# Four loads and transposes put elsewhere in a written order: attention with a relative bias, then a snake MLP

## The chip, the cores and the metric

The kernel runs on 1 core of one Trainium2 chip. The metric is the device time of one execution in microseconds (us); lower is better. Several executions are timed, and one more is run under the hardware profiler: its time, its span and its trace belong together.

## The reference

Attention over 8 batch elements, 8 heads, 576 positions and 64 channels a head, with a bias that depends on the distance of two positions alone; then, on the 8 x 576 = 4608 tokens of 512 channels that come out, a two-layer MLP of width 2048 with the activation h + sin(alpha h)^2 / alpha.

```python
scores = q @ k.transpose(0, 1, 3, 2) / np.sqrt(64) + bias      # bias[h, |i - j|], 32 buckets
attn = np.exp(scores - scores.max(-1, keepdims=True))
attn = attn / attn.sum(-1, keepdims=True)
x = (attn @ v).transpose(0, 2, 1, 3).reshape(4608, 512)
h = x @ w_in                                                   # 512 -> 2048
g = h + np.sin(alpha * h) ** 2 / alpha
out = g @ w_out                                                # 2048 -> 512
```

## The kernel before, in words

**Work and names.** The kernel records tasks, and a table called `ORDER` (a string, from line 343 on) lists them by short names, one after the other. Each task goes to one engine, and an engine runs its tasks in just that order, so each engine's queue is the table with the other engines' names left out. A number behind a slash is the PSUM bank (of eight), and a letter there another engine than the usual one. The names, with t the batch element (0 to 7), p the pair of heads (0 to 3), and b a block of 512 tokens (0 to 8):

- `n` t p kind: GpSimd loads the natural rows of k (kind 0) or q (kind 1) of one pair into a part of `xT` that is not used yet (L581, 144 KB). For t up to 2, TensorE turns them (`t` t p kind, L703) and a copy (`c`, L651 or L653) brings them to `kT` and `qT`. From t = 3 on, `g` stages a whole element in HBM (L608) and `k` turns it by a DMA of SyncE (L614).
- `v` t c and `y` t a: GpSimd loads the values. A `v` is 128 of the first 512 positions (L587, 128 KB), a `y` the last 64 positions for one head of each pair (L593, 32 KB). There are two sets of value tiles, so those of element t wait for the last product of element t - 2 that reads the set.
- `T`, `X`, `S`: scores on TensorE (L766, L720, L749, L725); `E` their exponential on ScalarE (L774), `B` the bias as a product on VectorE (L797 and neighbours).
- `A` t p w: probabilities times values for half the rows of a pair (L805 with `y`, then L810 with the four `v`); `L` t: the same for the last 64 rows of all pairs (L821). `N` and `NL` divide by the sum on VectorE (L842, L843), into tiles `xp` and `xl`.
- `Y` t p: SyncE turns an `xp` tile into `xT` by a DMA (L850), the columns of the first 512 positions of element t; `YL` t: two such DMAs (L861) bring its last 64 positions. For t = 0, TensorE and a copy do this.
- `I` b.f: 4 matmuls of the first layer (L887) that read 512 tokens of `xT`; `Z` the sine on ScalarE (L893), `Q` the square (L898 on ScalarE, L900 on VectorE), `G` the sum (L905). `O`: the second layer (L915), `W` its eviction (L651 or L653), `D` its store (L928). `wi` and `wo` load the weights (L598, L603).

**Order around the change.** TensorE does scores, products and both layers mixed, in one stream. Block 2 of the MLP, tokens 1024 to 1535, needs the last 128 tokens of element 1 and the first 384 of element 2: so `Y20` to `Y23` and `YL1`, but not `YL2`, whose tokens 1664 to 1727 belong to block 3.

**Queues.** GpSimd issues its loads one after the other, and so does SyncE its transposes and stores. Each of GpSimd's DMAs has one of eight semaphores in turn, and its issue waits until the DMA eight places before it has landed. A task that waits holds up all that stands behind it on its engine.

```python
    def turn_x(self, xcell, t, p):
        n0 = S * t
        self.nc.sync.dma_start_transpose(
            out=self.xT[:, p, n0:n0 + 512].rearrange("d (c s) -> d c s", c=4),
            in_=xcell["x"][:, :, :].rearrange("s c d -> s (c d)"))
```

Of the kernel before, what the change touches and what calls it, by code (L numbers as in the profile page):

```python
# [348 lines left out]
X00r/6 ET0300 n101 BT0210 BT0200 T0110/2 t111/5 n231 BT0000 ET0110 T0011/0 n130 t121/4 BT0001 c111
ET0011 n200 X01r/2 BT0010 c121 m0 EX00r X00q/0 BT0201 BT0110 m1 BT0101 EX01r BT0100 X01q/4 wi1  # L350
T0311/6 BX00r EX01q BT0011 A000/3 n210 BT0300 A010/2 EX00q n220 N000 A001/5 m3 BT0211 ET0311
t110/4 N010 m2 t101/3 T0111/0 c110/A N001 T0301/6 n120 ET0111 BX01r T0310/4 c101 n230 A020/2
ET0301 BT0111 wi2 A021/3 N020 T1000/0 ET0310 wi0 S0/7 N021 t130/6 y11 t231/2 ET1000 BT0301 T1001/4
BX00q A011/3 BT0311 wi3 ES0 c231 c130/A X10r/0 y10 ET1001 A030/7 BT0310 N011 v12 P00/6 BS0 EX10r
P02/2 A031/3 N030 v11 BX01q T1011/4 Y02/A N031 t220/7 ET1011 n221 T1100/0 Y00 T1300/2 c220 P01/6
ET1100 P03/5 Y01 t120/4 BT1011 t210/7 ET1300 T1010/0 c120 L0/6 ET1010 Y03 wo0 t230/4 NL0 t200/5
T1311/2 c200 T1301/0 I0.8/6 ET1311 c230 ET1301 S1/5 c210 X11r/2 v10 I0.0/4 BT1000 EX11r BT1100 v13
I0.3/7 ES1 Z0.0 BS1 BT1010 I0.9/5 BT1300 PL0/3 I0.7/2 YL0 n211 Z0.9 Q0.0 I0.1/3 wo1 Z0.3 Q0.9 G0.0
Z0.7 I0.12/1 v21 Q0.3/A G0.9 I0.2/4 wo2 Z0.8 G0.3 Q0.7/A I0.5/5 n201 Q0.8 Z0.2 G0.7 I0.14/7 Z0.1
Q0.2 Q0.1/A G0.8 I0.10/2 Z0.12 wo3 G0.2 I0.13/6 Q0.12/A BX10r g31 G0.1 Z0.10 I0.4/4 BT1001 Z0.14  # L360
# [24 lines left out]
BT3111 I2.0/3 BT3201 v43 ET3010 A300/1 I2.14/0 ET3200 BT3010 BT3301 N300 I2.5/7 Z2.0 D6 BT3101
BT3200 I2.13/6 BT3211 o4 I2.2/1 Z2.14 A310/5 Q2.14 Z2.2 D4 Q2.0 O7.12 Q2.2/A N310 I2.3/4 Z2.5 G2.0
I2.1/5 Q2.5/A G2.2 Z2.13 G2.14 A311/3 O7.14 G2.5 Z2.1 I2.6/1 Q2.13 Q2.1/A G2.13 Z2.3 I2.7/7 BS3
G2.1 I2.11/6 Z2.7 Q2.3 Z2.6 N311 I2.4/5 G2.3 Q2.7/A A301/3 Q2.6/A W7 I2.15/4 Z2.11 G2.6 D7 Q2.11/A
I2.12/2 G2.7 Z2.15 BX31r I2.9/1 Z2.4 G2.11 Q2.15/A BX30q I2.8/7 N301 Z2.9 Q2.4 Y30 I2.10/6 Q2.9/A
G2.15 Z2.8 G2.4 O8.0/3 Z2.12 D5 O8.2 G2.9 A330/0 Q2.8/A Z2.10 X40r/4 Y31 G2.8 A320/1 EX40r N330  # L390
O8.4 Q2.10 O8.6 N320 O9.0/7 G2.10 O9.2 T3310/0 Q2.12 T3210/4 O9.4 ET3310 G2.12 O10.0/6 ET3210
O10.2 O8.8 T3311/0 BT3210 T4200/4 O8.10 ET3311 A321/2 ET4200 BT3311 O8.12 O10.4 N321 T4300/0
BT3310 T4201/4 Y32 O8.14 ET4300 A331/2 W8 ET4201 L3/1 N331 T4011/4 Y33 NL3 v51 T4010/2 O9.6 ET4011
BX40r O9.8 y50 D8 ET4010 X41r/0 v50 O9.10 T4001/4 EX41r y51 T4211/2 O10.6 YL3 ET4001 v40 O10.8
O10.10 y40 ET4211 T4100/0 T4101/4 O9.12 v53 ET4100 O9.14 k50 v52 O10.12 W9 ET4101 O10.14 BT4200
T4000/0 T4110/2 T4301/4 ET4000 I3.3/7 ET4110 BT4000 S4/1 I3.15/0 BT4001 k51 ES4 W10 ET4301 A400/3
# [584 lines left out]
```

## Time and profile before

| what | value |
|---|---|
| timed runs, median of 3 | 380.35 us (380.34 to 381.17) |
| profiled execution, its own time | 381.76 us |
| its span | 379.9 us |
| TensorE (PE) busy | 365.4 us, 96% |
| ScalarE (ACT) busy | 310.5 us, 82% |
| VectorE (DVE) busy | 265.3 us, 70% |
| GpSimd (POOL) busy | 86.0 us, 23% |
| mean granted TensorE clock | 0.991 |

All times in the profile are counted from the start of the span. "Idle before" names the event that ended an engine's wait. A matmul's end is modelled, so rows of TensorE overlap a little. POOL's rows of L581, L587 and L593 are the issues of its loads; SPq rows are the issues of SyncE. The landing of a DMA is a number of its own, counted from the start of its issue. The granted clock is the share of full speed that TensorE had.

### The profile page before, as it was taken

To read this page: it belongs to the slowest core of one execution; us is meant where nothing else is said; L and a number is where in the kernel's file an instruction comes from. 1 tells how busy PE (TensorE), PEld (TensorE's weight loads), DVE (VectorE), ACT (ScalarE), POOL (GpSimd) and SP (SyncE) were. 2 spreads that over 40 slices of the span, in tenths; PEclk is the share of its full clock that TensorE was granted. 3 is DMA by queue.
4 is the path that set the end of the run, shared out by engine and by line. 5 is a ranking of instruction groups with operands and counts; after the bars stand their busy time and mean duration, and the time that the engine had idled before them with its cause. 6 is when DMAs were issued, how large, how long until landed. Compare 5 with 4: busy or idle time off the path is not lost.

```text
span 379.9 us, 9143 instructions
## 1 busy us (share of the span) xinstructions
PE 365.4 (96%) x3769; PEld 195.6 (51%) x3769; DVE 265.3 (70%) x613; ACT 310.5 (82%) x417; POOL 86.0 (23%) x104
## 2 busy tenths in 40 slices
PE   4879999999998899999999999999999999999996
PEld 3567445654464455544554555445654564444453
DVE  4789899639975496389754985596729866769412
ACT  5979998999899599899988989999899855686301
POOL 8894682048208000600000050500000000000000
PEclk9989999999999899999999999999999999999999
DMA  9999999999999992890254078980130032020005
GB/s 174 217 170 184 186 193 158 126 201 145 157 131 142 172 100 57 93 155 21 98 129 97 0 83 135 141 69 28 40 89 3 2 83 92 2 83 0 2 29 193
DMA packets 140889, 39.68 MB, mean 104 GB/s; under 512 B 126208, under 2 KB 136304, under 8 KB 140848
## 3 DMA queue, kind: packets, MB, share of 16 engines
q0 software_dynamic: 92864, 18.45, 60.0%
q1 hardware_dynamic: 46272, 18.61, 23.5%
q10 hardware_dynamic: 1712, 2.04, 1.6%
q8 instruction: 29, 0.48, 0.5%
q14 instruction: 12, 0.10, 0.1%
HBM read 36.89 MB, written 15.34 MB: 137 GB/s over the span
## 4 chain that ended last, share of the span: by engine, by line
PE 88%; DMA 6%; ACT 2%; POOL 1%; issue 1%; SPq 1%; DVE 1%; POOLq 0%
PE acc L915 33%; PE acc L887 31%; PE acc L810 8%; PE acc L766 8%; PE acc L805 2%; DMA xT<-xp 2%; DMA v<-in_v_dram 2%; PE acc L821 2%; DMA xT<-in_k_dram 2%; DMA toep<-e_sb 1%; ACT s L893 1%; PE acc L720 1%; PE acc L703 1%; POOL xT L581 1%; PE acc L749 1%
## 5 line engine op out<-in xcount | busy, mean ns | idle before, releaser
L915 PE MATMUL acc<-w_out,g 128*128 128x512 f16 (+1 forms) x592 | 144.3, 374 | 0.0
L887 PE MATMUL acc<-xT,w_in 128*128 128x512 f16 x576 | 135.8, 381 | 2.8 <-DMA xT<-xp 2.2
L774 ACT ACTIVATE u<-acc 128x1024 f16<-128x1024 f32 x128 | 123.7, 1034 | 12.2 <-PE acc L766 11.3
L893 ACT ACTIVATE s<-acc,alphaT 128x512 f16<-128x512 f32 x144 | 91.9, 682 | 23.6 <-PE acc L887 23.0
L905 DVE SCALAR_TENSOR_TENSOR g<-s,inv_a,acc 128x512 f16<-128x512 f16 x144 | 103.2, 742 | 7.3 <-ACT s L898 5.7
L887 PEld LDWEIGHTS <-w_in 128*128 128x128 f16 x576 | 55.3, 98 | 69.2 <-issue 6.5
L915 PEld LDWEIGHTS <-g 128*128 128x128 f16 x592 | 52.7, 98 | 59.0 <-issue 7.3
L797 DVE TENSOR_TENSOR u<-u,toep 128x256 f16<-128x256 f16 (+1 forms) x128 | 58.9, 489 | 19.8 <-ACT u L774 19.5
L587 POOL DMA_DIRECT2D v<-in_v_dram x32 | 30.9, 972 | 145.5 <-PE acc L821 79.0
L810 PE MATMUL acc<-v,u 128*128 128x65 f16 x1024 | 45.4, 196 | 0.5 <-DMA v<-in_v_dram 0.5
L900 DVE TENSOR_TENSOR s<-s 128x512 f16<-128x512 f16 x83 | 34.0, 419 | 17.0 <-ACT s L893 16.7
L810 PEld LDWEIGHTS <-u 128*128 128x128 f16 x1024 | 41.9, 99 | 4.9 <-issue 0.9
L766 PE MATMUL acc<-qT,kT 64*128 64x256 f16 x512 | 42.0, 278 | 1.5 <-DVE kT L653 1.0
L898 ACT ACTIVATE s<-s 128x512 f16<-128x512 f16 x61 | 37.9, 629 | 1.1
L653 DVE COPY outs<-acc 128x512 f32<-128x512 f32 (+1 forms) x24 | 16.2, 675 | 26.7 <-PE acc L915 25.4
L774 ACT ACTIVATE ux<-acc 128x1024 f16<-128x1024 f32 x32 | 32.4, 1035 | 1.8 <-PE acc L720 0.9
L766 PEld LDWEIGHTS <-kT 64*128 64x128 f16 x512 | 20.4, 96 | 22.8 <-issue 18.2
L842 DVE RECIPROCAL rden<-acc 128x4 f32<-128x4 f32 x72 | 12.7, 177 | 25.1 <-PE acc L810 18.7
L805 PE MATMUL acc<-vt,ux 128*128 128x130 f16 x128 | 28.8, 225 | 1.0 <-DMA vt<-in_v_dram 1.0
L843 DVE TENSOR_TENSOR xp<-acc,rden 128x256 f16<-128x256 f32 x64 | 27.2, 424 | 2.3
L651 ACT ACTIVATE outs<-acc 128x512 f32<-128x512 f32 (+1 forms) x13 | 7.6, 582 | 18.6 <-PE acc L915 18.5
L805 PEld LDWEIGHTS <-ux 128*128 128x128 f16 x128 | 12.7, 99 | 8.2 <-issue 2.8
(68 smaller groups left out, 199.2 us busy)
## 6 DMA issues: line engine op xcount, KB each, us to landing
out_dram<-outs SPq DMA_DIRECT2D x30, 256.0 KB, 2.3
v<-in_v_dram POOLq DMA_DIRECT2D x32, 128.0 KB, 6.8
staged_q<-in_q_dram POOLq DMA_DIRECT2D x5, 576.0 KB, 12.4
staged_k<-in_k_dram POOLq DMA_DIRECT2D x5, 576.0 KB, 14.9
w_in<-in_moe_w_in_dram POOLq DMA_DIRECT2D x4, 512.0 KB, 10.5
w_out<-in_moe_w_out_dram POOLq DMA_DIRECT2D x4, 512.0 KB, 10.6
xT<-in_q_dram POOLq DMA_DIRECT2D x11, 144.0 KB, 5.6
xT<-in_k_dram POOLq DMA_DIRECT2D x11, 144.0 KB, 5.9
```

The lines of the kernel that those rows point to most:

```text
L587: self.nc.gpsimd.dma_start(out=self.vs[t % 2][:, c, :, 0:D], in_=src)
L766: self.nc.tensor.matmul(out=s[:, o:o + 256], lhsT=self.kT[t % 2][r, p, 128 * c:128 * c + 128], rhs=self.qT[t % 2][r, p, 256 * w:256 * w + ...
L774: self.nc.scalar.activation(out=c["u"], in_=c["s"], func=AF.Exp, scale=0.125)
L797: self.nc.vector.tensor_tensor(out=io, in0=io, in1=m, op=ALU.mult)
L805: nc.tensor.matmul(out=c["av"][:, 130 * j:130 * j + 130], lhsT=cx["u"][:, o:o + 128], rhs=vt[:, p, :], start=True, stop=True, skip_group_c ...
L810: nc.tensor.matmul(out=c["av"][:, 130 * j + 65 * a:130 * j + 65 * a + 65], lhsT=cells[ch // 2]["u"][:, o:o + 128], rhs=vv[:, ch, 2 * p + a ...
L887: self.nc.tensor.matmul(out=c["h"], lhsT=self.w_in[:, j, 128 * f:128 * f + 128], rhs=self.xT[:, j, 512 * b:512 * b + 512], start=(j == 0), ...
L893: self.nc.scalar.activation(out=c["s"], in_=c["h"], func=AF.Sin, scale=self.alphaT[:, f:f + 1])
L898: self.nc.scalar.activation(out=c["s"], in_=c["s"], func=AF.Square)
L900: self.nc.vector.tensor_tensor(out=c["s"], in0=c["s"], in1=c["s"], op=ALU.mult)
L905: self.nc.vector.scalar_tensor_tensor(out=self.g[b][:, f, :], in0=c["s"], scalar=self.inv_a[:, f:f + 1], in1=c["h"], op0=ALU.mult, op1=ALU ...
L915: self.nc.tensor.matmul(out=c["mo"], lhsT=self.g[b][:, f, 128 * (tau % 4):128 * (tau % 4) + 128], rhs=self.w_out[:, f, at], start=(f == 0) ...
```

## The change

The diff rewrites most lines of `ORDER`, but on each engine only three queue places differ; TensorE, ScalarE and VectorE have the same order as before. In the words of the table, around one of them:

```diff
-T3101/0 NL2 v42 T3211/6 T3100/4 ET3101 O4.8 YL2 v41 O4.10 ET3100 O4.12 y41 O7.0/2 ET3211 BT3100
-X31q/0 v31 T3111/4 O7.2 ET3111 Y20 g70 O7.4 O4.14 EX31q X30q/4 W4 T3201/6 O7.6 EX30q BT3011 k41
+NL2 v42 T3211/6 T3100/4 ET3101 Y23 O4.8 v41 O4.10 ET3100 O4.12 y41 O7.0/2 ET3211 BT3100 X31q/0 v31
+Y20 T3111/4 O7.2 ET3111 g70 O7.4 O4.14 EX31q X30q/4 W4 T3201/6 O7.6 YL2 EX30q BT3011 S3/3 g61 O7.8
```

SyncE, in the middle of the program; `xp` tiles are those of `Y`, `xl` those of `YL`, and the numbers behind the names count recorded tiles. Before, from `k40` to `k41`:

```order
L614 DMA_TRANSPOSE kT0_65<-staged_k 128x4x576
L850 DMA_TRANSPOSE xT_77<-xp_2068 128x4x128
L861 DMA_TRANSPOSE xT_77<-xl_2131 128x2x64 x2
L850 DMA_TRANSPOSE xT_77<-xp_1928 128x4x128
L614 DMA_TRANSPOSE qT0_67<-staged_q 128x4x576
```

And now, in the same place:

```order
L614 DMA_TRANSPOSE kT0_65<-staged_k 128x4x576
L850 DMA_TRANSPOSE xT_77<-xp_2067 128x4x128
L850 DMA_TRANSPOSE xT_77<-xp_1928 128x4x128
L861 DMA_TRANSPOSE xT_77<-xl_2130 128x2x64 x2
L614 DMA_TRANSPOSE qT0_67<-staged_q 128x4x576
```

`Y20` (xp_1928) stands ahead of both DMAs of `YL2` instead of behind them.

GpSimd, early in the program, as a difference; `xT<-in_k` is `n110`, the `v_71` and `vt_73` rows are `v03`, `v01`, `y01` and `v02` of element 0:

```order
 L581 DMA xT<-in_q_dram 96x2x384 x2
 L662 DMA toep<-e_sb 128x1x384 x4
-L581 DMA xT<-in_k_dram 96x2x384
 L587 DMA v_71<-in_v_dram 128x8x64 x2
 L593 DMA vt_73<-in_v_dram 64x4x64
 L587 DMA v_71<-in_v_dram 128x8x64
+L581 DMA xT<-in_k_dram 96x2x384
 L581 DMA xT<-in_q_dram 96x2x384 x2
```

`n110` is issued behind the four value loads instead of ahead of them.

GpSimd, in the middle; `v_71` and `vt_73` belong to even elements, `v_72` and `vt_74` to odd ones:

```order
 L608 DMA staged_q<-in_q_dram 4608x1x64
-L587 DMA v_71<-in_v_dram 128x8x64
+L587 DMA v_71<-in_v_dram 128x8x64 x2
+L593 DMA vt_73<-in_v_dram 64x4x64
 L587 DMA v_72<-in_v_dram 128x8x64
 L593 DMA vt_74<-in_v_dram 64x4x64
 L587 DMA v_72<-in_v_dram 128x8x64
 L593 DMA vt_74<-in_v_dram 64x4x64
-L587 DMA v_71<-in_v_dram 128x8x64
-L593 DMA vt_73<-in_v_dram 64x4x64
 L587 DMA v_72<-in_v_dram 128x8x64 x2
 L587 DMA v_71<-in_v_dram 128x8x64
```

`v40` and `y40` follow `v43` at once; before, they stood behind `v51`, `y50`, `v50` and `y51`, which belong to the next element.

More of the change, by code (lines that the diff above doesn't have):

```diff
@@ L349 @@
[L349 to L360, printed above, removed]
@@ L385 @@
[L385 to L396, printed above, removed]
@@ L421 @@
[L421 to L423 removed]
+t011/7 ET0210 j1/G t010/6 c011 T0211/0 ET0201 T0200/2 c010 j3 at/7 v03 ET0200 av T0101/4 t100/6
+v01 ET0101 t031/7 c100 t030/3 t131/2 y01 ET0211 c031 T0100/4 v02 c030 ET0100 n110 c131 T0300/0
+n101 X00r/6 BT0210 ET0300 BT0200 n231 BT0000 T0110/2 n130 BT0001 t111/5 ET0110 n200 T0011/0 c111
@@ new lines @@
+A221/2 BS2 BT2311 EX20q O4.0/3 N221 O4.2 BT3300 T3301/0 ET3011 T3000/4 A201/2 BX21q ET3301 Y22
+A230/7 N201 A231/6 ET3000 N230 X30r/0 N231 O4.4 k40 EX30r O4.6 BX20q T3001/4 L2/2 ET3001 T3101/0
+NL2 v42 T3211/6 T3100/4 ET3101 Y23 O4.8 v41 O4.10 ET3100 O4.12 y41 O7.0/2 ET3211 BT3100 X31q/0 v31
+Y20 T3111/4 O7.2 ET3111 g70 O7.4 O4.14 EX31q X30q/4 W4 T3201/6 O7.6 YL2 EX30q BT3011 S3/3 g61 O7.8
+BT3000 ET3201 O7.10 BT3110 X31r/0 BX30r BX31q ES3 T3200/4 BT3001 EX31r BT3111 T3010/6 BT3201 v43
+ET3010 I2.0/3 k41 v40 ET3200 BT3010 A300/1 BT3301 y40 I2.14/0 Z2.0 N300 BT3101 I2.5/7 BT3200
```

137 lines of the change are left out of this document (77 added, 60 removed).

## The prediction

> **What bounds the kernel now.** I read the page first: the busy shares, the clock and the chain of waits.
>
> ```profile
> PE 365.4 (96%) x3769; PEld 195.6 (51%) x3769; DVE 265.3 (70%) x613; ACT 310.5 (82%) x417; POOL 86.0 (23%) x104
> ...
> PEclk9989999999999899999999999999999999999999
> ...
> PE 88%; DMA 6%; ACT 2%; POOL 1%; issue 1%; SPq 1%; DVE 1%; POOLq 0%
> ```
>
> TensorE sets the time: it is busy for 96% of the span and makes 88% of the chain. So a load is worth only what TensorE waits for it. The clock row has its two dips to 8, at about 19 to 28 us and 124 to 133 us. The second view is TensorE's own waits.
>
> ```profile
> PE acc L887 <- DMA xT<-xp: 2.2, 1, 2.2
> PE acc L805 <- DMA vt<-in_v_dram: 1.0, 1, 1.0
> ...
> PE acc L810 <- DMA v<-in_v_dram: 0.5, 1, 0.5
> ```
>
> These are all its waits for loads and transposes: 2.2 us once for a transposed `xp` tile, and 1.0 and 0.5 us for the first values. The third view is the chain around the longest one (start, length, what).
>
> ```profile
> 115.70 1.18 SPq L861
> ...
> 116.93 1.23 SPq L861
> ...
> 118.21 6.32 DMA xT<-xp
> ...
> 124.66 1.50 PE acc L887 x4
> ...
> 143.53 0.86 PE acc L915 x4
> ...
> 162.66 0.97 PE acc L887 x4
> ```
>
> SyncE issues the two DMAs of `YL2`, and only then `Y20`, which lands 6.3 us later; block 2's first matmuls wait for it. (The last two rows serve below.) The timeline shows what stands around.
>
> ```profile
> 114.38 1.22 SPq L850 DMA_TRANSPOSE xT<-xp  x1
> ...
> 115.18 1.79 POOL L587 DMA_DIRECT2D v<-in_v_dram  x2 [16.02 <-PE acc L821]
> ...
> 117.58 0.92 POOL L587 DMA_DIRECT2D v<-in_v_dram  x1
> ...
> 121.90 0.61 PE L766 MATMUL acc<-qT,kT 64*128 64x256 f16 x8
> ...
> 124.66 1.50 PE L887 MATMUL acc<-xT,w_in 128*128 128x512 f16 x4 [2.16 <-DMA xT<-xp]
> ...
> 128.83 0.69 ACT L893 ACTIVATE s<-acc,alphaT 128x512 f16<-128x512 f32 x1 [1.93 <-PE acc L887]
> ```
>
> TensorE is ready at 121.90 + 0.61 = 122.5 and stands still until 124.66. Then it is slow: the stretches of one microsecond behind the wait have these granted clocks (the figure ahead of the last two).
>
> ```profile
> 125.00:126.00 1.00, 1.00 (x5) 0.35 (x3) 0.00 (x0) 1.00 (x1) 0.00 (x0) 0.54 2.01 123
> 126.00:127.00 1.00, 1.00 (x18) 1.00 (x17) 0.00 (x0) 0.88 (x2) 0.00 (x0) 0.50 1.16 98
> 127.00:128.00 1.00, 1.00 (x8) 0.44 (x6) 0.67 (x3) 0.00 (x0) 0.00 (x0) 0.50 1.81 151
> 128.00:129.00 1.00, 1.00 (x5) 0.40 (x4) 1.00 (x3) 0.17 (x1) 0.00 (x0) 0.76 2.36 156
> ```
>
> TensorE is busy throughout, so the clock that is missing is time: 0.46 + 0.50 + 0.50 + 0.24 = **1.70 us**. The wait costs 2.16 + 1.70 = 3.86 us in all, if the drop is its consequence.
>
> **The change, first part: `Y20` ahead of `YL2`.** `Y23`'s issue ends at 114.38 + 1.22 = 115.60. `Y20` doesn't need `NL2`, so it goes out there instead of at 118.21, 2.6 us earlier. `YL2`'s issues follow at about 116.9 and 118.1, and `k41` goes out where it did, since the same three issues stand ahead of it. `YL2` has no reader before block 3, whose matmuls stand in the chain at 162.66: some 40 us cover its delay of 1.2 us. When does `Y20` land? Here are three single landings: of `Y23`, of the first half of `YL2` and of `v31` (issued at 117.58).
>
> ```profile
> xT<-xp SPq DMA_TRANSPOSE x1, 2.5
> xT<-xl SPq DMA_TRANSPOSE x1, 4.8
> v<-in_v_dram POOLq DMA_DIRECT2D x1, 128.0 KB, 6.8
> ```
>
> `Y23`, ahead of the value loads, took 2.5 us; the first `YL2`, issued at 115.70 in the place that `Y20` now gets, took 4.8; `Y20`, amid the loads, took 6.3. So it lands between 118.1 and 122.0, and I take 120.5, by the neighbour in the same place. All of these lie ahead of 122.5: **the 2.16 us go**.
>
> What is late next? Behind `I2.0` TensorE's order has `A300`, which reads `v31`; that one lands at 117.58 + 6.8 = 124.4, by a load that isn't moved. `I2.0` is four matmuls, 0.86 us at full clock by the row at 143.53, which are four of the same shape. `A300` begins at 122.5 + 0.9 = 123.4, does its first two or three small products and stands until 124.4: **a new wait of about 1.0 us**. From below it is nothing, if `v31` lands sooner because fewer transposes lie beside it; from above 1.0 and as much as `v31` is delayed by `Y20`'s larger transfer, 1.5 us more at most by the spread from 4.8 to 6.3 us. I take 1.0.
>
> Does the clock still drop? TensorE would stand for 1.0 us instead of 2.16 us. The early dip (below) stands behind a stretch with waits of 1.04 and 0.54 and more small ones; a single us is less than their sum. I take it that the drop goes: **+1.70**. ScalarE doesn't take this back: ahead of the block's second sine, at 128.83, it waits 1.93 us for TensorE, and this idle time and what follows it absorb the shift. First part: 2.16 + 1.70 - 1.0 = **2.9 us**.
>
> **Second part: `n110` behind four value loads.** GpSimd's issues, and TensorE's wait:
>
> ```profile
> 12.63 0.67 POOL L581 DMA_DIRECT2D xT<-in_k_dram  x1
> ...
> 16.38 0.89 POOL L587 DMA_DIRECT2D v<-in_v_dram  x1 [0.60 <-DMA toep<-e_sb]
> ...
> 17.26 1.28 POOL L581 DMA_DIRECT2D xT<-in_q_dram  x2
> ...
> 21.76 0.23 PE L805 MATMUL acc<-vt,ux 128*128 128x130 f16 x1 [1.04 <-DMA vt<-in_v_dram]
> ...
> 25.71 0.86 PE L703 MATMUL acc<-ident,xT 96*64 96x96 f16 x24
> ...
> 26.36 0.65 ACT L651 ACTIVATE kT<-acc 128x576 f16<-128x576 f16 x1 [2.43 <-PE acc L703]
> ```
>
> Each value load goes out a place earlier, the last one, `v02`, also without its wait for a bias load: at about 15.05 instead of 16.38. If its landing moved as its issue, the gain would be 1.33 us. But the DMA engines are full here, and a load ahead costs its share of them:
>
> ```profile
> 21.00:22.00 1.00, 0.24 (x3) 0.20 (x4) 1.00 (x4) 1.00 (x3) 1.00 (x2) 1.00 1.28 187
> ```
>
> At 187 GB/s `n110`'s 144 KB take 0.79 us, the nearest price. The lower end is the distance of two landings, `v02`'s in the chain and `n101`'s, issued at 17.26:
>
> ```profile
> 16.38 6.17 DMA v<-in_v_dram
> xT<-in_q_dram POOLq DMA_DIRECT2D x1, 144.0 KB, 5.6
> ```
>
> 22.55 and 22.9, so 0.35 us. I take **0.7 us**. It isn't lost behind: ScalarE stands idle for 2.43 us before the copy of `t110`.
>
> `n110` goes out at 16.38 now, since it inherits the wait for the bias load; with `v02`'s 6.2 us it lands at 22.6. TensorE turns it at 25.71 - 0.7 = 25.0, so 2.4 us cover it. Behind that, `n101` and all later loads keep their places. The first layer's weights come next:
>
> ```profile
> 26.39 1.51 POOL L598 DMA_DIRECT2D w_in<-in_moe_w_in_dram  x2
> DMA to landing us min/median/max: 8.4/10.5/11.4
> 40.38 2.76 PE L887 MATMUL acc<-xT,w_in 128*128 128x512 f16 x12
> ```
>
> The second of these loads goes out at 27.14 and lands by 38.5; `I0.0` needs it at 40.38 - 0.7 = 39.7. That still holds.
>
> **Third part: `v40`, `y40` ahead of the next element's.** They go out at about 124 instead of 158, as their tiles are free since `L2`. Their first reader is `A400`:
>
> ```profile
> 164.59 0.22 PE L805 MATMUL acc<-vt,ux 128*128 128x130 f16 x1
> ```
>
> It has no idle time ahead of it, so there is nothing to gain, and 40 us cover the two loads; without this cover `A400` would stand a us for each us that they are late. Their 160 KB lie behind the staged loads, whose transposes come later still. **0 us.**
>
> **Sum.** 2.9 + 0.7 = 3.6 us. Against the profiled execution's own time, 381.76 us (a span of 379.9 and 1.9 around it), this is 378.2. That execution was 1.4 us over the median of the timed runs; from the median, 380.35, the forecast is **376.8 us**. TensorE waits for no load behind 130 us, so the shift reaches the end.
>
> **The rivals.** (1) *More goes than that.* The early dip in the clock also vanishes, and `v31` lands in time.
>
> ```profile
> 20.00:30.00 10.00, 8.33 (x184) 7.05 (x185) 8.39 (x24) 7.57 (x10) 8.29 (x17) 0.83 1.22 169
> ```
>
> A clock of 0.83 over 10 us is 1.7 us missing, as in the other dip. For it: TensorE stands 0.7 us less. Against: about half of the two waits stays. With the dip gone 375.1, with no wait for `v31` either 374.1.
>
> (2) *The clock's drop is not the wait's.* If half clock at 125 to 129 comes from something else, or if the remaining 1.0 us also brings it, the first part is worth 2.16 - 1.0 = 1.2, and the time is 380.35 - 1.2 - 0.7 = 378.5. For it: the pause is short. Against: both dips stand right behind the two places where TensorE waits for loads, and there is no third one. [...]
>
> (3) *The transposes starve.* `Y20` lands no earlier, since the DMA engines serve the value loads first, as its own 6.3 us beside `Y23`'s 2.5 suggest. It would have to land at 124.5 still, 8.9 us after its issue. Then only the early 0.7 is left, 379.7, or nothing, 380.35.
>
> (4) *Slower: `v31` is pushed back.* At `A300`, if `Y20`'s transfer slows the value loads. `A300` now starts at about 126.1 behind `I2.0`; from there on each us of delay costs one. With the early 0.7 it decides when `v31` lands behind 126.8, 9.2 us after its issue instead of 6.8. `v43`, which lies behind the staged loads, shows how far this can go:
>
> ```profile
> v<-in_v_dram POOLq DMA_DIRECT2D x1, 128.0 KB, 16.0
> ```
>
> At 128.8 the time would be 2 us longer, 382.3. Against: `v31` keeps its place ahead of the staged loads.
>
> **How the numbers follow.** Forecast 0.42, rival 1 0.20, rival 2 0.16, rival 3 0.15, rival 4 0.07. A measurement of this kernel tells about 0.3% from no change: 379.2 to 381.5. Forecast and rivals 1 and 2 lie below, 0.78; rival 3 within, 0.15, with a little of rival 4; slower 0.06. The range takes in the forecast, rivals 1 and 2, and the better end of rival 3: 374.3 to 379.7; about 0.15 is left out.
>
> **What would show it.** In the changed profile, `Y20` is issued at about 115 and takes under 6 us; TensorE's wait for `xT<-xp` is gone, a wait of L810 for `v` of about 1 us stands at 123 to 124, and the clock is 1.00 from 124 to 130. The first L805 starts at about 21.0, and ScalarE's idle 2.43 us are some 0.7 shorter. It is wrong if a wait for `xT<-xp` stays, if the clock is 0.50 there, or if L703 at 25 waits for `n110`.

## The result, and the profile after

| | before | after |
|---|---|---|
| timed runs, median (range, count) | 380.83 us (380.34 to 381.35, 6) | 377.85 us (376.38 to 378.84, 6) |
| profiled execution, its own time | 381.76 us | 377.51 us |
| its span | 379.9 us | 375.7 us |
| its mean granted clock | 0.991 | 1.000 |

The ratio is 0.9921, with a 95% interval of 0.9899 to 0.9943: 3.0 us less (2.2 to 3.8). The profiled executions lie 4.25 us apart. That the two figures differ is the most instructive part of this case.

The page of the kernel after: busy TensorE, the granted clock, the chain.

```profile
PE 363.5 (97%) x3769; PEld 193.9 (52%) x3769; DVE 265.2 (71%) x613; ACT 311.0 (83%) x417; POOL 86.6 (23%) x104
...
PEclk9999999999999999999999999999999999999999
...
PE 87%; DMA 5%; POOL 4%; ACT 2%; issue 1%; DVE 1%; POOLq 0%
```

Both dips of the clock row are gone. The only wait of TensorE for a load or a transpose that its list of waits still has is this one:

```profile
PE acc L810 <- DMA v<-in_v_dram: 0.3, 1, 0.3
```

The timeline around it: two rows of SyncE, one of GpSimd, four of TensorE, one of ScalarE.

```profile
113.51 2.54 SPq L850 DMA_TRANSPOSE xT<-xp  x2
116.14 2.48 SPq L861 DMA_TRANSPOSE xT<-xl  x2
...
116.87 0.90 POOL L587 DMA_DIRECT2D v<-in_v_dram  x1
...
121.19 0.61 PE L766 MATMUL acc<-qT,kT 64*128 64x256 f16 x8
121.73 1.04 PE L887 MATMUL acc<-xT,w_in 128*128 128x512 f16 x4
...
122.66 0.19 PE L810 MATMUL acc<-v,u 128*128 128x65 f16 x1
123.11 0.37 PE L810 MATMUL acc<-v,u 128*128 128x65 f16 x7 [0.26 <-DMA v<-in_v_dram]
...
127.27 0.69 ACT L893 ACTIVATE s<-acc,alphaT 128x512 f16<-128x512 f32 x1 [0.51 <-PE acc L887]
```

The first row is `Y23` and `Y20` one behind the other, and `YL2` follows. `I2.0` (121.73) now starts right behind the scores of 121.19. `A300` still waits for `v31`, but for 0.26 us. The single landings of `Y20` and of `v31`, in us from their issues at 114.82 and 116.87:

```profile
xT<-xp SPq DMA_TRANSPOSE x1, 4.9
v<-in_v_dram POOLq DMA_DIRECT2D x1, 128.0 KB, 6.2
```

So `Y20` is there at 119.7, two us ahead of its reader, and `v31` at 123.1. The clock behind this place, over 8 us and by the figure ahead of the last two, and the early stretch for which the profile before showed 0.83:

```profile
122.00:130.00 8.00, 7.74 (x71) 4.23 (x70) 6.13 (x18) 7.40 (x11) 2.59 (x4) 1.00 1.63 193
20.00:30.00 10.00, 8.00 (x195) 6.12 (x195) 9.29 (x25) 9.00 (x12) 9.66 (x18) 1.00 1.11 159
```

The early place, one row each of GpSimd (`n110`), TensorE (the first product), ScalarE and VectorE:

```profile
17.20 0.66 POOL L581 DMA_DIRECT2D xT<-in_k_dram  x1 [1.17 <-DMA toep<-e_sb]
...
21.40 0.22 PE L805 MATMUL acc<-vt,ux 128*128 128x130 f16 x1 [0.24 <-ACT ux L774]
...
24.46 0.65 ACT L651 ACTIVATE kT<-acc 128x576 f16<-128x576 f16 x1 [0.36 <-PE acc L703]
...
26.47 0.29 DVE L783 TENSOR_TENSOR ux<-ux,mt 128x256 f16<-128x256 f16 x1 [0.29 <-POOL mt L668]
```

The first product waits for ScalarE and no longer for a value, ScalarE for only 0.36 us ahead of its copy, and VectorE for a mask of GpSimd. Setting the same TensorE instructions of the two traces beside each other, the kernel after is ahead by 1.9 us at 24 us, by only 0.7 from 35 to 121 us, by 2.9 at `I2.0`, and by 4.3 from `A400` to the end. What was won at 24 us is mostly gone at 35.

### The profile page after: what moved, and what is told of

The parts are those of the page before. It is cut to its first block, busy times and chain, and to the rows that moved or that the text cites. A ratio compares the mean times of both kernels' runs of the same rounds, so it can differ in the third digit from the quotient of the medians.

```text
span 375.7 us, 9143 instructions
## 1 busy us (share of the span) xinstructions
PE 363.5 (97%) x3769; PEld 193.9 (52%) x3769; DVE 265.2 (71%) x613; ACT 311.0 (83%) x417; POOL 86.6 (23%) x104
## 4 chain that ended last, share of the span: by engine, by line
PE 87%; DMA 5%; POOL 4%; ACT 2%; issue 1%; DVE 1%; POOLq 0%
PE acc L915 33%; PE acc L887 31%; PE acc L766 8%; PE acc L810 8%; PE acc L805 2%; POOL xT L581 2%; DMA toep<-e_sb 2%; DMA v<-in_v_dram 2%; PE acc L821 2%; DMA xT<-in_k_dram 2%; ACT s L893 1%; PE acc L720 1%; POOL mt L668 1%; PE acc L703 1%; PE acc L749 1%
## 5 line engine op out<-in xcount | busy, mean ns | idle before, releaser
L810 PE MATMUL acc<-v,u 128*128 128x65 f16 x1024 | 44.0, 193 | 0.6 <-DVE u L797 0.3
L810 PEld LDWEIGHTS <-u 128*128 128x128 f16 x1024 | 40.2, 97 | 5.7 <-issue 0.8
```

Source lines behind the costliest of these rows:

```text
L810: nc.tensor.matmul(out=c["av"][:, 130 * j + 65 * a:130 * j + 65 * a + 65], lhsT=cells[ch // 2]["u"][:, o:o + 128], rhs=vv[:, ch, 2 * p + a ...
```

## The experiments

All were timed against the kernel before on their own chip, in three batches. A *dip* in what follows is one stretch of 3.41 us at a granted clock of 0.50; it takes 0.0045 from the mean clock of an execution (half of 3.41 us in a span of 380; the profile before, with two, has 0.991), so each timed run's mean clock tells how many it had. It doesn't tell where in the run they lay, nor how long TensorE was slow at the start: in the profile before, 24 matmuls of L703 took 1.17 us at 10.81, and 48 took 1.21 us at 13.42.

| kernel | us, median (range, runs) | ratio, 95% interval | runs with 0, 1, 2 or more dips |
|---|---|---|---|
| before, first batch | 380.74 (378.00 to 383.46, 35) | | 20, 11, 4 |
| y20_alone | 378.59 (376.69 to 382.01, 12) | 0.9960 (0.9926 to 0.9994) | 7, 5, 0 |
| n110_alone | 379.66 (379.06 to 382.92, 12) | 1.0003 (0.9971 to 1.0036) | 7, 5, 0 |
| v40_alone | 380.35 (378.65 to 382.74, 12) | 0.999 (0.996 to 1.002) | 5, 4, 3 |
| fill_wait | 381.85 (379.75 to 382.75, 12) | 1.0029 (1.0002 to 1.0055) | 6, 6, 0 |
| before, second batch | 380.74 (378.94 to 383.68, 29) | | 11, 14, 4 |
| y20_late | 387.56 (386.57 to 389.12, 6) | 1.0187 (1.0139 to 1.0236) | 0, 0, 6 |
| fill_v40 | 380.40 (378.42 to 381.78, 12) | 0.9985 (0.9955 to 1.0016) | 6, 6, 0 |
| y20_n110 | 378.47 (377.11 to 381.07, 12) | 0.9939 (0.9911 to 0.9968) | 10, 1, 1 |
| masks_v31 | 378.20 (377.70 to 379.26, 12) | 0.9949 (0.9923 to 0.9975) | 9, 3, 0 |
| before, third batch | 381.08 (378.58 to 381.91, 11) | | 5, 4, 2 |
| y20_v40 | 377.34 (376.87 to 378.03, 6) | 0.9907 (0.9879 to 0.9934) | 3, 3, 0 |
| after_again | 378.03 (376.95 to 378.09, 6) | 0.9920 (0.9894 to 0.9946) | 5, 1, 0 |
| after_v31 | 377.25 (376.70 to 378.35, 6) | 0.9908 (0.9882 to 0.9935) | 5, 1, 0 |

### The first move alone

```diff
-T3101/0 NL2 v42 T3211/6 T3100/4 ET3101 O4.8 YL2 v41 O4.10 ET3100 O4.12 y41 O7.0/2 ET3211 BT3100
-X31q/0 v31 T3111/4 O7.2 ET3111 Y20 g70 O7.4 O4.14 EX31q X30q/4 W4 T3201/6 O7.6 EX30q BT3011 k41
+T3101/0 NL2 v42 T3211/6 T3100/4 ET3101 O4.8 Y20 YL2 v41 O4.10 ET3100 O4.12 y41 O7.0/2 ET3211 BT3100
+X31q/0 v31 T3111/4 O7.2 ET3111 g70 O7.4 O4.14 EX31q X30q/4 W4 T3201/6 O7.6 EX30q BT3011 k41
```

> Only Y20 is moved ahead of YL2, the rest is as before. Theory: TensorE's wait of 2.16 us for xT<-xp goes, with it the half clock behind it (1.70 us), and a wait for v31 of some 0.3 us comes; so about 3.5 us less than before, and the wait for the first values (1.0 and 0.5 us) and the early dip in the clock stay. Rival, the clock falls for another reason: half clock stays at 125 to 129 us and only about 1.9 us are gained. Rival, the transposes starve behind the value loads: no gain.

Measured: 1.5 us by the ratio (0.2 to 2.8), so less than the 3.5 that I expected; but 378.23 us for the profiled execution, 3.5 less than the one before. TensorE's waits for loads in it, and its clock row:

```profile
PE acc L810 <- DMA v<-in_v_dram: 0.7, 2, 0.5
PE acc L805 <- DMA vt<-in_v_dram: 0.2, 1, 0.2
...
PEclk9989999999999999999999999999999999999999
```

The wait for `xT<-xp` is gone with this move alone. In its place stand 0.49 us for `v31` and 0.2 us for `y40` at `A400`, and no dip at 125. The early dip, which this move cannot reach, is there as before.

### The second move alone

```diff
-t011/7 ET0210 t010/6 j1/G c011 T0211/0 ET0201 T0200/2 j3 c010 at/7 n110 ET0200 av T0101/4 v03
-t100/6 t031/7 ET0101 c100 t030/3 v01 t131/2 c031 ET0211 T0100/4 y01 c030 ET0100 v02 c131 T0300/0
+t011/7 ET0210 t010/6 j1/G c011 T0211/0 ET0201 T0200/2 j3 c010 at/7 ET0200 av T0101/4 v03
+t100/6 t031/7 ET0101 c100 t030/3 v01 t131/2 c031 ET0211 T0100/4 y01 c030 ET0100 v02 n110 c131 T0300/0
```

> Only n110 is moved behind the four value loads, the rest is as before. Theory: the values land 0.6 to 1.5 us sooner, the early dip in the clock goes, TensorE is 1.8 us ahead at the turn of n110, but GpSimd's masks come later and take over 1 us back, so 0.7 us are left from 28 us on; the wait of about 2.2 us for xT<-xp and the half clock behind it stay. About 0.7 us less than before. Rival, the early clock is worth its 1.7 us in full: 1.8 to 2.4 us less.

Measured: no difference by the ratio, 1.0003 (0.9971 to 1.0036), which by itself leaves room for the expected 0.7 us. In its profile (379.47 us) neither dip appears, though the wait for `Y20` is there. The row of TensorE is that wait; the two rows below are windows of 3.41 us, with TensorE's busy time as the first figure behind the length:

```profile
123.08 1.02 PE L887 MATMUL acc<-xT,w_in 128*128 128x512 f16 x4 [1.67 <-DMA xT<-xp]
...
119.03:122.45 3.42, 2.38 (x20) 1.01 (x18) 2.87 (x9) 3.42 (x5) 3.42 (x3) 1.00 1.60 114
122.45:125.86 3.41, 2.78 (x29) 1.62 (x30) 1.58 (x6) 3.38 (x5) 0.26 (x1) 1.00 1.55 145
```

I laid these windows on the grid of 3.41 us that the clock's own steps in this trace give. The wait falls across two of them, and TensorE is busy for 70 and 82% of them.

### The third move alone

```diff
-BT3111 I2.0/3 BT3201 v43 ET3010 A300/1 I2.14/0 ET3200 BT3010 BT3301 N300 I2.5/7 Z2.0 D6 BT3101
+BT3111 I2.0/3 BT3201 v43 v40 y40 ET3010 A300/1 I2.14/0 ET3200 BT3010 BT3301 N300 I2.5/7 Z2.0 D6 BT3101
...
-BX40r O9.8 y50 D8 ET4010 X41r/0 v50 O9.10 T4001/4 EX41r y51 T4211/2 O10.6 YL3 ET4001 v40 O10.8
-O10.10 y40 ET4211 T4100/0 T4101/4 O9.12 v53 ET4100 O9.14 k50 v52 O10.12 W9 ET4101 O10.14 BT4200
+BX40r O9.8 y50 D8 ET4010 X41r/0 v50 O9.10 T4001/4 EX41r y51 T4211/2 O10.6 YL3 ET4001 O10.8
+O10.10 ET4211 T4100/0 T4101/4 O9.12 v53 ET4100 O9.14 k50 v52 O10.12 W9 ET4101 O10.14 BT4200
```

> Only v40 and y40 are moved ahead of the next element's value loads, the rest is as before. Theory: no product of element 4 waited for them, so no change, at most 0.2 us at the first reader (164.59 us before). Rival, the loads crowd out the transposes of k41 and the staged loads around 124 us: slower by up to 1 us.

Measured: 0.999 (0.996 to 1.002), so within 0.4% of nothing. Its profile shows `Y20`'s wait once more, and the window of 3.41 us in which the wait lies, with the one behind it:

```profile
124.43 1.02 PE L887 MATMUL acc<-xT,w_in 128*128 128x512 f16 x4 [1.75 <-DMA xT<-xp]
...
122.10:125.51 3.41, 1.66 (x20) 0.91 (x20) 1.56 (x6) 3.39 (x5) 3.39 (x4) 1.00 1.40 110
125.51:128.92 3.41, 3.41 (x32) 1.75 (x29) 2.77 (x8) 2.12 (x3) 0.00 (x0) 1.00 1.92 152
```

TensorE is busy for 1.66 of 3.41 us, 49%, and the clock stays at 1.00. In the profile before, the window with the wait had 37% and the next one ran at 0.50:

```profile
121.66:125.07 3.41, 1.25 (x12) 0.53 (x11) 1.83 (x7) 3.39 (x6) 2.16 (x2) 1.00 1.35 111
125.07:128.48 3.41, 3.41 (x25) 1.99 (x24) 1.15 (x4) 1.81 (x2) 0.00 (x0) 0.50 1.74 128
```

So the wait at this place brings a dip only in a part of the executions. The three profiles fit the reading that it depends on how long the wait is (1.67 to 2.16 us here) and on where the grid falls across it.

### The wait filled with work

The kernel before, with nine more matmuls in the place where TensorE stood; their result is overwritten.

```diff
         c["h"] = self.acc[:, bank, :]
+        for i in range(9 if (b, f) == (2, 0) else 0):
+            self.nc.tensor.matmul(out=c["h"], lhsT=self.w_in[:, i % 4, 0:128],
+                                  rhs=self.xT[:, i % 4, 512:1024], start=True, stop=True)
```

> As before, with the order unchanged; ahead of the first matmul of block 2 stand nine matmuls of 128x512 into the same bank, which the block's own first matmul overwrites: TensorE works through the 2.16 us in which it waited for Y20. Theory, the half clock behind the wait is the wait's consequence: I2.0 still starts at about 124.6, the clock is 1.00 from 125 to 129, and the time is about 1.7 us less than before although work was added. Rival, the clock falls there for another reason: 0.50 from 125 to 129 as before, and no change in the time.

Measured: 1.0029 (1.0002 to 1.0055), so slower, by 1.1 us. At 125 it did what it was made for: the window with the filled wait is busy throughout, and no dip follows. That alone proves little, since two executions with the wait unfilled had no dip there either.

```profile
121.11:124.52 3.41, 3.41 (x32) 1.79 (x31) 0.84 (x4) 3.39 (x4) 1.15 (x2) 1.00 1.38 134
```

But 40 us later stands a new wait. The rows are TensorE's, the landing of `y40`, which was issued at 155.95, and two windows:

```profile
163.49 0.22 PE L805 MATMUL acc<-vt,ux 128*128 128x130 f16 x1 [2.25 <-DMA vt<-in_v_dram]
...
vt<-in_v_dram POOLq DMA_DIRECT2D x1, 32.0 KB, 7.4
...
160.28:163.69 3.41, 1.16 (x14) 0.46 (x10) 2.63 (x6) 3.38 (x5) 0.00 (x0) 1.00 1.34 117
163.69:167.10 3.41, 3.41 (x25) 1.76 (x22) 1.89 (x5) 0.39 (x1) 0.00 (x0) 0.50 2.35 154
```

`A400` waits 2.25 us for `y40`, and the window with this wait (34% busy) is followed by a dip. In the profile before, `y40` was issued at 159.31 and landed 5.1 us later, at 164.45, when its reader began at 164.59:

```profile
vt<-in_v_dram POOLq DMA_DIRECT2D x1, 32.0 KB, 5.1
```

From landing to reader are 0.14 us. That is no reserve: in fill_wait, where `A400` plainly waits, the same 0.14 us lie between the landing (163.35) and the start, so before the change too `A400` started when `y40` let it. GpSimd's rows of the kernel before show what sets the time of the load; they are `v51` and `y40`:

```profile
155.43 0.89 POOL L587 DMA_DIRECT2D v<-in_v_dram  x1 [31.62 <-PE acc L821]
...
159.31 0.69 POOL L593 DMA_DIRECT2D vt<-in_v_dram  x1
```

`v51` waits for `L3`, TensorE's last product of element 3, and `y40` goes out behind it and four other loads, 4.1 us after the end of `L3` in all six profiles with this order. So it moves along with whatever is gained ahead of `L3`. What differs is how long it takes to land: 5.1, 5.3, 5.4, 5.6, 5.9 and 7.4 us (before, y20_alone, n110_alone, y20_n110, y20_late, fill_wait). In the seven profiles in which `v40` and `y40` are moved, `A400` starts 9.25 us behind the end of `L3`; in these six it starts later than that by 0.14, 0.35, 0.40, 0.57, 0.94 and 2.41 us, 0.80 on average. This pointed at the third move, so the next run adds just that.

### The same with the third move

```diff
-BT3111 I2.0/3 BT3201 v43 ET3010 A300/1 I2.14/0 ET3200 BT3010 BT3301 N300 I2.5/7 Z2.0 D6 BT3101
+BT3111 I2.0/3 BT3201 v43 v40 y40 ET3010 A300/1 I2.14/0 ET3200 BT3010 BT3301 N300 I2.5/7 Z2.0 D6 BT3101
...
-BX40r O9.8 y50 D8 ET4010 X41r/0 v50 O9.10 T4001/4 EX41r y51 T4211/2 O10.6 YL3 ET4001 v40 O10.8
-O10.10 y40 ET4211 T4100/0 T4101/4 O9.12 v53 ET4100 O9.14 k50 v52 O10.12 W9 ET4101 O10.14 BT4200
+BX40r O9.8 y50 D8 ET4010 X41r/0 v50 O9.10 T4001/4 EX41r y51 T4211/2 O10.6 YL3 ET4001 O10.8
+O10.10 ET4211 T4100/0 T4101/4 O9.12 v53 ET4100 O9.14 k50 v52 O10.12 W9 ET4101 O10.14 BT4200
```

> fill_wait (nine more 128x512 matmuls in I2.0's wait, whose result is overwritten) and v40, y40 right behind v43, as the third move has them. Everything is still computed. Theory (fill_wait lost its gain because y40 landed 7.4 us after its issue at 155.95, and A400 waited 2.25 us for it and set off half a clock window): A400 has no wait for vt now, there is no dip at 164 to 168, and the median is 379.0 to 380.0 us, 2 us below fill_wait's 381.85 and at or a little below the kernel before, for the nine matmuls take 2.1 us of a wait of 2.2. Rival (the nine matmuls cost their time wherever A400 stands, and the third move is worth nothing): 381 to 382 us, as fill_wait.

Measured: 380.40 us, 0.9985 (0.9955 to 1.0016). `A400` starts without a wait (162.68), and no dip follows:

```profile
121.75 2.12 PE L887 MATMUL acc<-xT,w_in 128*128 128x512 f16 x9
124.52 1.04 PE L890 MATMUL acc<-xT,w_in 128*128 128x512 f16 x4 [0.66 <-DMA xT<-xp]
...
162.68 0.22 PE L805 MATMUL acc<-vt,ux 128*128 128x130 f16 x1
```

The median is 1.5 us below that of fill_wait, 0.4 us above what the theory allowed and 0.6 below the rival; the two ratios' intervals still touch (0.9955 to 1.0016 and 1.0002 to 1.0055). The mechanism is shown by the rows; its size in the median is only made likely. Both kernels had a dip in 6 of their 12 timed runs, so that the gain is one of dips isn't shown.

### `Y20` later still

```diff
-X31q/0 v31 T3111/4 O7.2 ET3111 Y20 g70 O7.4 O4.14 EX31q X30q/4 W4 T3201/6 O7.6 EX30q BT3011 k41
+X31q/0 v31 T3111/4 O7.2 ET3111 g70 O7.4 O4.14 EX31q X30q/4 W4 T3201/6 O7.6 EX30q BT3011 k41 Y20
```

> The kernel before with Y20 issued behind k41 instead of ahead of it. Everything is still computed. k41's issue takes 4.6 us in the profile before, so Y20 goes out at about 122.8 instead of 118.2, and I2.0's wait for xT<-xp grows from 2.2 to about 6.7 us in the profile. Theory (the half clock is the wait's: one free-running window of 3.41 us at 0.5 follows a window in which TensorE was busy for 0.42 or less): a wait of over 6 us leaves at least one such window whatever the phase, so every execution shows a dip there, the mean clock is 0.9955 or lower in all runs (before: 20 of 35 runs without a dip), and the time is that of the executions without a dip, 379.9, + 4.5 for the wait + 0.5 to 1.7 for the clock behind it = 385 to 386 us. Rival (the dips come by chance and not from the wait): runs without a dip are as frequent as before, and the median is 380.7 + 4.5 = 385.2 us. The mean clock of the runs tells them apart, not the time.

Measured: 387.56 us, over both theories' times, and all six runs have two dips or more (mean clocks of 0.991, 0.991, 0.982, 0.991, 0.982 and 0.987). The wait and four windows around it:

```profile
127.68 1.89 PE L887 MATMUL acc<-xT,w_in 128*128 128x512 f16 x4 [7.05 <-DMA xT<-xp]
...
118.88:122.29 3.41, 1.75 (x14) 0.66 (x12) 2.39 (x9) 3.41 (x6) 3.04 (x2) 1.00 1.45 124
122.29:125.71 3.42, 0.00 (x0) 0.00 (x0) 0.34 (x2) 2.01 (x2) 0.00 (x0) 1.00 2.15 187
125.71:129.12 3.41, 1.44 (x4) 0.59 (x5) 0.00 (x0) 0.00 (x0) 0.00 (x0) 0.50 1.53 241
129.12:132.53 3.41, 3.41 (x25) 1.83 (x23) 1.79 (x5) 0.81 (x2) 0.00 (x0) 0.50 2.46 157
```

The window with no work at all is followed by one at 0.50, and that one, 42% busy, by another. Half clock reaches from the wait's end at 127.68 to 132.53, 4.85 us, which costs 2.4 us; with 7.05 - 2.16 = 4.9 us more of waiting that is 7.3 us, and over the batch's 379.4 us of runs without a dip 386.7 us. Its profiled execution took 386.57. That every run had its dips, where 11 of 29 runs before had none, speaks for the wait as their cause and against chance. My expectation had one window too few.

### The kernel after without its third move

```diff
-ET3010 I2.0/3 k41 v40 ET3200 BT3010 A300/1 BT3301 y40 I2.14/0 Z2.0 N300 BT3101 I2.5/7 BT3200
+ET3010 I2.0/3 k41 ET3200 BT3010 A300/1 BT3301 I2.14/0 Z2.0 N300 BT3101 I2.5/7 BT3200
...
-D8 ET4010 X41r/0 v50 O9.10 T4001/4 EX41r y51 T4211/2 O10.6 YL3 v53 ET4001 O10.8 O10.10 v52 ET4211
+D8 ET4010 X41r/0 v50 O9.10 T4001/4 EX41r y51 v40 y40 T4211/2 O10.6 YL3 v53 ET4001 O10.8 O10.10 v52 ET4211
```

> The kernel after without its third move: v40 and y40 stand behind v51, y50, v50 and y51 again, as before. Everything is still computed. Theory (the third move has a small worth, since y40 landed only 0.14 us ahead of A400 in the profile before, and A400 waited 0.2 us for it in the profiles of the first and of the second move alone): a wait of L805 for vt of 0.2 to 1 us near 160, and a median of 378.0 to 378.6 us, 0.2 to 0.8 over the kernel after. Rival (worth nothing, as forecast): no wait for vt, and the same time as after, 377.5 to 377.9 us.

Measured: 378.47 us, 0.9939 (0.9911 to 0.9968), beside 0.9921 and 0.9920 for the kernel after: 0.7 us, well inside the intervals. `A400` does wait:

```profile
160.29 0.22 PE L805 MATMUL acc<-vt,ux 128*128 128x130 f16 x1 [0.41 <-DMA vt<-in_v_dram]
```

By its distance from `L3`, `A400` is 0.57 us late here. So the third move takes away what the old order costs at `A400`, 0.14 to 2.41 us in the six profiles. A worth of 0.7 us in the median fits that; it isn't shown, since the kernels ran on different chips and the intervals hold nothing as well.

### Masks together, and `v31` sooner

```diff
-m0 t121/4 BT0010 ET0011 m1 X01r/2 c121 EX00r wi1 X00q/0 BT0201 BT0110 X01q/4 BT0101 EX01r n210
-T0311/6 BT0100 n220 BX00r EX01q BT0011 A000/3 m3 BT0300 EX00q A010/2 m2 N000 A001/5 BT0211 ET0311
+m0 t121/4 BT0010 ET0011 m1 m3 m2 X01r/2 c121 EX00r wi1 X00q/0 BT0201 BT0110 X01q/4 BT0101 EX01r n210
+T0311/6 BT0100 n220 BX00r EX01q BT0011 A000/3 BT0300 EX00q A010/2 N000 A001/5 BT0211 ET0311
...
-NL2 v42 T3211/6 T3100/4 ET3101 Y23 O4.8 v41 O4.10 ET3100 O4.12 y41 O7.0/2 ET3211 BT3100 X31q/0 v31
+NL2 v31 v42 T3211/6 T3100/4 ET3101 Y23 O4.8 v41 O4.10 ET3100 O4.12 y41 O7.0/2 ET3211 BT3100 X31q/0
```

> The kernel after, with v31 issued ahead of v42, v41 and y41 on GpSimd, and with the eight mask copies (m0 to m3) in one row, so that m3 and m2 stand ahead of wi1, n210 and n220. Everything is still computed. Theory: v31 goes out at about 114.5 instead of 116.9 and lands by 120, so A300's 0.26 us wait is gone; VectorE's wait of 0.29 us for a mask at 26.5 is gone too. What the second move lost between 26 and 28 us (1.84 of gain fell to 0.51) comes back only by about 0.3, since VectorE is otherwise without a gap from 22.4 to 29. Together 0.4 to 0.6 below after: 377.0 to 377.4 us. Rival (the masks are what held the second move back): the whole 1.3 us come back as well, 376.0 to 376.4 us. Rival on the other side: wi1 goes out 2 us later, and I0.0 at about 39 waits for it; then the gain goes and the time is 377.9 us or more.

Measured: 378.20 us, 0.9949 (0.9923 to 0.9975), so no gain shows in the time. It is a time that the last rival allowed, but TensorE's list of waits has none for `w_in`. `A300` doesn't wait for `v31` any more (after_v31, below, has this alone). VectorE's rows at the masks:

```profile
22.74 0.29 DVE L783 TENSOR_TENSOR ux<-ux,mt 128x256 f16<-128x256 f16 x1 [1.39 <-POOL mt L668]
...
26.69 0.28 DVE L783 TENSOR_TENSOR ux<-ux,mt 128x256 f16<-128x256 f16 x1
```

The wait for a mask at 26.5 is gone as meant, but the second mask product starts at 26.69 instead of 26.47, since the first one waited 1.39 us instead of 0.24. The eight copies in a row took GpSimd until 25.1, and a mask still holds VectorE, only at another place. So neither gain came, and whether the masks are what held the second move back stays open. Between the two rows VectorE has no gap; what it is late with at 22.7 it is still late with at 29.

### The kernel after without its second move, once more whole, and with `v31` sooner

The three share a chip. In y20_v40:

```diff
-t011/7 ET0210 j1/G t010/6 c011 T0211/0 ET0201 T0200/2 c010 j3 at/7 v03 ET0200 av T0101/4 t100/6
-v01 ET0101 t031/7 c100 t030/3 t131/2 y01 ET0211 c031 T0100/4 v02 c030 ET0100 n110 c131 T0300/0
+t011/7 ET0210 j1/G t010/6 c011 T0211/0 ET0201 T0200/2 c010 j3 at/7 n110 v03 ET0200 av T0101/4 t100/6
+v01 ET0101 t031/7 c100 t030/3 t131/2 y01 ET0211 c031 T0100/4 v02 c030 ET0100 c131 T0300/0
```

> The kernel after without its second move: n110 stands ahead of v03 v01 y01 v02 again, as before. Everything is still computed. Theory (the second move is worth nothing: the early wait for vt of 1.04 us in the profile before is not there in the profiles of the first move alone, the third alone, fill_wait and fill_v40, in which n110 is not moved either, and VectorE's L779 of about 29 us starts at 28.6 to 29.9 in most profiles with either order): the time is that of the kernel after in the same batch within 0.4 us, about 377.9 us, and L779 starts at 28.5 to 29.5. Rival (the second move is worth 0.7 us, as forecast): 378.6 us, 0.7 over after.

> The kernel after once more, for a comparison with y20_v40 and after_v31 on the same chip. Everything is still computed. Its first runs gave 377.85 us and a ratio of 0.992. Theory (first move about 2.2 us with 0.6 us of clock on average, the second nothing, the third 0.1 to 0.5): a ratio of 0.992 to 0.994 and 377.8 to 378.6 us, and a mean clock over its runs of 0.998 or more, for dips now come at the early place only. Rival (all three terms as forecast, 3.6 us): a ratio of 0.9905.

In after_v31 only the move of `v31` in the third pair of lines of masks_v31 is made.

> The kernel after, with v31 issued ahead of v42, v41 and y41 on GpSimd. Everything is still computed. Theory: v31 lands about 2 us sooner, well ahead of A300, so the wait of L810 for v behind 123 us (0.26 us in the profile of after) is gone, and nothing else moves: the time is that of after_again less 0.0 to 0.3 us. Rival (v42, v41 and y41, or Y20, which share the queues with it, are late instead): a wait of I2.0 for xT<-xp of 0.2 us or more, and no gain.

Measured: 0.9907, 0.9920 and 0.9908, all within each other's intervals, and the forecast in full, 0.9905, lies in them too. Without the second move the kernel is not slower (by the medians 0.7 us faster, where I had expected 0.4 either way), though its profiled execution has the wait for the first `y` that the move is about, and reaches L779 later than expected. TensorE's row, and VectorE's L779, the first task behind the crowded stretch:

```profile
22.17 0.23 PE L805 MATMUL acc<-vt,ux 128*128 128x130 f16 x1 [0.79 <-DMA vt<-in_v_dram]
...
30.41 0.28 DVE L779 TENSOR_TENSOR ux<-ux,toep 128x256 f16<-128x256 f16 x1
```

The same row in two executions in which `n110` also stands ahead of the values, the kernel before and fill_v40, and then in one with the move, n110_alone:

```profile
29.96 0.28 DVE L779 TENSOR_TENSOR ux<-ux,toep 128x256 f16<-128x256 f16 x1
```

```profile
28.72 0.28 DVE L779 TENSOR_TENSOR ux<-ux,toep 128x256 f16<-128x256 f16 x1
```

```profile
29.37 0.29 DVE L779 TENSOR_TENSOR ux<-ux,toep 128x256 f16<-128x256 f16 x1
```

Over all 13 profiles: with `n110` ahead, 28.60 to 30.64, median 29.12 (seven: y20_late, fill_v40, fill_wait, y20_alone, before, y20_v40, v40_alone); with it behind, 29.08 to 29.46, median 29.31 (six). The wait for the first `y` is in two of the seven, and they are among the three latest; four of the other five stand at 28.60 to 29.12, no later than nearly all with the move. The 0.7 us by which the profile after was ahead from 35 to 121 us lie within the 2 us by which executions of the old order differ, and can't be put down to the new one.

The early dip follows the order more closely: four of the seven have it (before, y20_alone, v40_alone, y20_v40), and none of the six. So the move may well take it away, which isn't shown. Three of these four are the three latest at L779, by 0.5 to 1.2 us, and y20_alone isn't late; in the time nothing came of it. That a slow TensorE needn't cost anything so early shows in y20_n110:

```profile
20.17 0.69 PE L703 MATMUL acc<-ident,xT 96*64 96x96 f16 x12
...
23.19 0.22 PE L805 MATMUL acc<-vt,ux 128*128 128x130 f16 x1 [0.52 <-ACT ux L774]
```

Twelve such matmuls of L703 take 0.45 us in the profile after, at 18.12. By the trace's clock, TensorE is at full speed only from 21.46 on here (24 of these matmuls take 0.70 us at 25.07), against 11.4 to 14.4 in the other twelve profiles (12.43 before, 13.61 after). Its first product starts at 23.19 instead of 21.40, but L779 at 29.40 all the same.

In after_again `A300` waits 0.64 us for `v31`; in after_v31 it doesn't wait:

```profile
123.42 0.37 PE L810 MATMUL acc<-v,u 128*128 128x65 f16 x7 [0.64 <-DMA v<-in_v_dram]
```

```profile
123.88 0.22 PE L805 MATMUL acc<-vt,ux 128*128 128x130 f16 x1
123.93 0.41 PE L810 MATMUL acc<-v,u 128*128 128x65 f16 x8
```

0.26 to 0.64 us can be had there, then. The median is 0.8 us lower, which these six runs each don't tell from nothing (0.9882 to 0.9935 against 0.9894 to 0.9946).

## Why the prediction was right or wrong, point by point

The forecast was 376.8 us in a range of 374.3 to 379.7; the runs gave 377.85. About half of the difference is the kernel before, which came to 380.83 us beside the runs after, not 380.35. The gain was forecast at 3.6 us and measured at 3.0 (2.2 to 3.8), so the total doesn't refute the sum. Its terms do, and that they add up so nearly is in part luck: the clock and `n110` were put too high, the new wait at `A300` too, which counts the other way, and the third part was worth more than nothing.

- **`Y20` ahead of `YL2`, the wait of 2.16 us.** Right. It was to go out at about 115 and land at 120.5; it went out at 114.82 and landed at 119.7, and in none of the seven profiles with this move does `I2.0` wait as before (0.2 us in y20_n110, nothing in the others). Rival 3, the starving transposes, falls, and so does rival 4: `v31` landed sooner, 6.2 us after its issue instead of 6.8.
- **The new wait at `A300`.** Right in place and cause, too large: 1.0 us was forecast, 0.26 to 0.64 us measured in four profiles and none in y20_n110. I had kept `v31`'s landing at 124.4; in the new order it was 123.1.
- **The clock, "+1.70".** This is the term that was mis-sized. In the profiles the dip at 125 went with the wait, as said: no profile with `Y20` ahead has it, and y20_late, with a longer wait, has a longer one. But the profile before was one of the few executions with two dips: of 75 timed runs of that kernel 36 had none, 29 one and 10 two, 0.65 on average, and the first two batches' runs without a dip are 1.3 and 1.7 us shorter than those with one. Of 12 runs of the kernel after, 10 had none and 2 had one, 0.17 on average. By that the clock is worth 0.48 dips of 1.3 to 1.7 us, 0.6 to 0.8 us and not 1.70. This is an estimate, and rather too high: it counts early dips too, and runs with a dip can be longer because the wait itself was. With `Y20` ahead, where the profiles show early dips alone, runs with one were 1.5 us longer on average in y20_alone, and no longer than the others in y20_v40 and masks_v31. The failed step is the last one of the sum: "from the median, 380.35, the forecast is 376.8" took terms of an execution that was itself 1.4 us over the median and subtracted them from the median whole. Runs with two dips lie 0.9, 1.8 and 0.4 us over the medians of their batches, so a good part of those 1.4 us was most likely the dips themselves.
- **`n110` behind four value loads, 0.7 us.** Not found in the median, though the profile after seemed to bear it out to the tenth. n110_alone gave 1.0003, and the kernel after gave nothing up without the move. The wait that it removes is in two of seven executions with the old order, and VectorE's row of work from 22 to 29 us takes up what is left. "It isn't lost behind" was the step that failed: ScalarE's 2.43 us did shrink, to 0.36, but VectorE's next task had no such reserve. In rival 1 I had taken the vanished early dip as a consequence of the wait; executions without the move, fill_v40 for one, show no early dip either, and y20_alone shows one with 0.2 us of waiting for values.
- **`v40`, `y40`, 0 us.** Wrong. "It has no idle time ahead of it, so there is nothing to gain" was the step that failed: `A400` began when `y40` had landed, with a wait too short for the list, and in the five other profiles with the old order it was later still. "TensorE waits for no load behind 130 us" was true of the one list alone. The term was worth 0.14 to 2.41 us in the profiles. By the medians it is 0.4 us alone (1.5 less to 0.8 more), 0.7 by y20_n110 and 1.5 between fill_wait and fill_v40; these agree in sign, but no single one is clear of nothing.
- **Rival 2, the clock's drop is not the wait's.** It falls by y20_late, where all six runs have two dips or more, and by the dip behind fill_wait's new wait, at 163.7 us, where no other profile has one. Waits of 2.16 and 2.25 us had a dip behind them (before, fill_wait). Half clock in mid-program came in pieces of 3.41 us (125.07 to 128.48 before, 163.69 to 167.10 in fill_wait), or two in a row (125.71 to 132.53 in y20_late), and no dip followed a wait of 1.67 us across two windows (n110_alone) or one of 1.75 us (v40_alone).

The terms as measured, all estimates from a few profiles: 1.67 to 2.16 us for the wait (n110_alone, v40_alone, before), less 0 to 0.64 at `A300`, at most 0.6 to 0.8 for the clock, and 0.80 on average for `y40`. By the means that is 1.86 - 0.36 + 0.80 = 2.3 us without the clock and up to 3.1 with it; the ratio says 3.0 (2.2 to 3.8). How much of it is the clock's stays open.

## What to carry to other kernels

Before a term is taken from the one profiled execution, ask whether the timed runs have it: their mean clocks are listed beside their times, and a clock event that only some of them show is worth its share and no more. The same holds for a wait that one profile doesn't show. "No idle time ahead" in front of a reader says nothing about reserve: look up when its load landed, and what released the load's issue, since a load tied to an earlier product moves along with every gain and can be late again. And a tenth of agreement between two profiles is no proof of a cause: several executions of the old order showed the same gain without the move.

## What the runs showed of the hardware

- In mid-program the half clock came in whole windows of 3.41 us. In the profile before, the two dips begin at 22.67 and 125.07, which are 102.40 us apart, 30 times 3.413. Such a grid lies elsewhere in each execution: around the late wait, windows begin at 121.66, 122.10 and 122.45 us (before, v40_alone, n110_alone). The windows ahead of a dip, by their rows, were 0, 34, 37 and 42% busy around the late waits (y20_late, fill_wait, before, y20_late); late windows of 49 and 51% (v40_alone, y20_late) had no dip behind them. Early, amid many small matmuls, dips followed windows of 41, 45, 52 and 61% (before, y20_v40, v40_alone, y20_alone), where masks_v31's of 60% and y20_late's of 63% were followed by none. So busy time alone does not give one limit; what is counted stays open.
- One 32 KB load of values took 5.1 to 7.4 us (before, fill_wait) from issue to landing in six executions with the same neighbours in its queue. What made it so was not found.
- In the five executions in which TensorE is listed as waiting for this load, its matmul began 0.14 us after the landing (163.35 and 163.49 in fill_wait). The same 0.14 us in the profile before (164.45 and 164.59), with no wait listed, gave away that it had waited there too.
